# Where the attention weights are divided by their sums: before the product with v, or after it

## The chip, the core and the metric

The kernel runs on one core of a Trainium2 chip. The metric is device time in microseconds from start to end of one execution, the median of several runs. TensorE is called PE in the rows, its weight loads PEld, VectorE DVE, ScalarE ACT, GpSimd POOL, SyncE SP.

## What is computed

Three layers run one after the other over 2304 tokens (4 batches of 576). The change lies in the first of them, attention that keeps the 32 largest scores of each row:

```python
scores = scale * np.matmul(q, k.transpose(0, 1, 3, 2))       # (4, 8, 576, 576), head size 64
kth = np.partition(scores, -32, axis=-1)[..., -32:-31]
scores = np.where(scores >= kth, scores, -1000000000.0)
scores = scores - np.max(scores, axis=-1, keepdims=True)
attn = np.exp(scores)
attn = attn / (np.sum(attn, axis=-1, keepdims=True) + 1e-09)
out = np.matmul(attn, v)
x = out.transpose(0, 2, 1, 3).reshape(2304, 512)
```

The second layer is a gated one (512 to 1536 to 512, its two input matrices multiplied as a sigmoid gate and a value), the third sends each token to two of eight experts (512 to 1024 to 512) and adds their weighted results.

## The kernel before

**Order of the work.** A planner (`Plan`, L48) is handed every operation with an engine, a duration, a priority, what it depends on and which buffers it takes and returns. It plays the operations through, engine by engine, and calls the function that issues an operation at the moment at which its turn has come by these durations. So each engine's queue is in the order that the planner found, fixed when the kernel is built; on the chip each engine works its queue off in order and waits where an input or a buffer is not there yet. The number of buffers of each kind is in `CAPS` (L173): four tiles of weights (`e`), three PSUM banks `tp`, two buffers `pt` for turned weights, and so on.

**Units.** Attention is cut into units. For the first 512 queries of a batch a unit is 128 queries of two heads: two tiles of 128 x 576 scores (64 units). The last 64 queries of a batch make units of one tile, whose lower half is one head and upper half the other (16 units). There are 80 units and 144 tiles.

**The steps of a unit** (`attention`, L319), each with its engine:

- PE multiplies q and k in two fp16 halves into PSUM (L345, L348), ACT copies the scores to SBUF (`sS`, L353).
- DVE finds the 24 largest of each row (L362 to L371), POOL works out a bias (L387), ACT takes a sign (L396), POOL removes the largest (L401, L402), DVE finds the 32nd (L409), POOL notes it (L411). ACT takes the exponential of all scores (`e`, L379).
- DVE puts what is below the 32nd to zero and sums the rest of each row in the same instruction (L425, the mask); the sum lands in column 34 of `u.m`.
- POOL adds 1e-9 to the sums (L429), DVE takes the reciprocal of the two columns (L431), POOL multiplies each tile of 128 x 576 weights with it (L434).
- PE turns each tile in 128-column blocks: four blocks into one `tp` bank (L452) and the last 64 columns of both tiles into another (L471). ACT copies them to SBUF (L459, L473).
- PE multiplies v with the turned weights (L483): the result stands as 64 head columns x 128 queries for two heads, the heads in the partitions 0 to 63 and 64 to 127. ACT makes the high fp16 half of x from it (L489), DVE the low one (L492).

**Around it.** Before and beside the early units the weights of the second layer are split into fp16 halves (`weight_piece`, L279 to L290, on ACT, DVE and POOL). When all units of a chunk of 256 or 128 tokens are done, the second layer runs for it (`moe1`: L519 to L558 on PE, L526 and L533 on ACT, L529 on DVE, L536 on POOL), so that its matmuls lie between those of later units. The third layer follows when all tokens are routed (L790, L816 on PE).

Of the kernel before, what the change touches and what calls it, by code (L numbers as in the profile page):

```python
# [11 lines left out]
FT = mybir.dt.float32  # L12
# [4 lines left out]
AF = mybir.ActivationFunctionType  # L17
OP = mybir.AluOpType
# [10 lines left out]
SQ, SX, SG, SV, SO, SX2, S1, S2 = 2.0 ** 6, 2.0 ** 6, 2.0 ** 4, 2.0 ** 5, 2.0 ** 6, 2.0 ** 7, 2.0 ** 6, 2.0 ** 6  # L29
# [18 lines left out]
class Plan:  # L48
# [10 lines left out]
    def op(self, eng, dur, prio, fn, deps=(), alloc=(), use=(), lat=None, chain="", dma=False):  # L59
        o = Unit()  # L60
        o.eng, o.dur, o.prio, o.fn, o.lat = eng, dur, prio, fn, LAT[eng] if lat is None else lat
        o.alloc, o.use, o.next, o.same = list(alloc), list(alloc) + list(use), [], []
        o.n, o.id, o.dma = 0, len(self.ops), dma
        deps = list(deps)
        for t in {h.tag for h in o.alloc}:
            deps.append(self.last.get((eng, chain, t)))
            self.last[eng, chain, t] = o
        for d in deps:
            if d is not None:
                (d.same if d.eng == eng and not d.dma else d.next).append(o)  # L70
                o.n += 1
        for h in o.use:
            h.left += 1
        self.ops.append(o)
        return o
# [51 lines left out]
def attention_moe_kernel(ctx: ExitStack, tc: tile.TileContext, qT, kT, v, w_gate, w_val, w_out,  # L127
# [3 lines left out]
    V, A, P, G = nc.vector, nc.scalar, nc.tensor, nc.gpsimd  # L131
# [6 lines left out]
    ident = const.tile([128, 128], FT, name="ident")  # L138
# [26 lines left out]
    for b in range(B):  # L165
        G.iota(tok[:, 4 * b:4 * b + 4], pattern=[[128, 4]], base=b * S, channel_multiplier=1,
               allow_small_or_imprecise_dtypes=True)
        d = slice(64 * (b % 2), 64 * (b % 2) + 64)
# [2 lines left out]
    nst = const.tile([128, N // 128, E], FT, name="nst")  # L171

    CAPS = dict(st=3, w=0, tb=4, khl=5, v=5, sS=6, sg=2, m=5, y=4, e=4, pt=2, xch=2, xrem=1, th=2, g=10, x2=2,  # L173
                ps=1, tp=3, mm=3)

    def layers(fast):
        outer = ExitStack()
# [7 lines left out]
        small = p1.enter_context(tc.tile_pool(name="small", bufs=2))  # L185
        psum = p1.enter_context(tc.tile_pool(name="psum", bufs=1, space=PSUM))
        p1.enter_context(tc.manual_schedule())
        plan = Plan(CAPS)
        op = plan.op

        def tile_of(tag, shape, dt, name=None):
            pool = psum if tag in ("ps", "tp", "mm") else stage if tag == "st" else work
            return pool.tile(shape, dt, name=name or tag, bufs=CAPS[tag])
# [125 lines left out]
        def attention(u, kqr, prio):  # L319
            R = range(u.nt)  # L320
            n = 128 if u.nt == 2 else 64
            ch = u.ch
            T = [Unit() for _ in R]
# [11 lines left out]
            for t in R:  # L335
# [18 lines left out]
                a = op("PE", 0.5 if u.nt == 2 else 0.5, prio, qk, kqr.done, alloc=[hp_], use=[kqr.h])  # L354
# [27 lines left out]
            if fast:  # L382
# [8 lines left out]
                for t in R:  # L391
# [11 lines left out]
                    a = op("ACT", 0.78, prio, sg, [c2], alloc=[hg], use=[T[t].hs])  # L403
# [20 lines left out]
            def mask(t):  # L424
                return lambda: V.scalar_tensor_tensor(T[t].e, T[t].s, T[t].m[:, 31:32], T[t].e, op0=OP.is_ge, op1=OP.mult,  # L425
                                                      accum_out=T[t].m[:, 34:35])
            mk = [op("DVE", 0.75, prio, mask(t), [r4, exs[t]], use=[T[t].hs, T[t].he]) for t in R]

            iv = op("POOL", 0.12, prio - 1, lambda: G.tensor_scalar(u.m[:, :, 35], u.m[:, :, 34], 1e-9, 1.0, op0=OP.add, op1=OP.mult),  # L429
                    mk)  # L430
            iv = op("DVE", 0.08, prio - 1, lambda: V.reciprocal(u.m[:, :, 33], u.m[:, :, 35]), [iv])  # L431

            def norm(t):
                return lambda: G.tensor_scalar(T[t].e, T[t].e, u.m[:, t, 33:34], 1.0, op0=OP.mult, op1=OP.mult)  # L434
            nm = [op("POOL", 0.74, prio, norm(t), [iv], use=[T[t].he, u.hm]) for t in R]


            if u.coff == 0 and u.hp == 0:
                def opened():
                    ch.x = [work.tile([128, 4, 128 if ch.rem else 256], FH, name=f"{tag}{c}", bufs=CAPS[tag])[:, :, :ch.n]  # L440
                            for c in range(2)]
                tag = "xrem" if ch.rem else "xch"
                ch.h = plan.tile(tag)
                ch.open = op("SP", 0.0, prio, opened, alloc=[ch.h], lat=0.0)
            hpt = plan.tile("pt")
            evs = []

            def tr(t):
                def f():
                    T[t].pp = tile_of("tp", [128, 4, 128], FT)  # L450
                    for kb in range(4):
                        P.transpose(T[t].pp[:, kb, :], T[t].e[:, kb * 128:(kb + 1) * 128], ident)  # L452
                return f

            def ev(t):
                def f():
                    if t == 0:
                        u.pt = work.tile([128, NK, u.nt, 128], FT, name="pt", bufs=CAPS["pt"])
                    A.activation(u.pt[:, 0:4, t, :], T[t].pp, AF.Copy)  # L459
                return f  # L460
            for t in R:
                ht = plan.tile("tp")
                a = op("PE", 0.44, prio, tr(t), [nm[t], ch.open], alloc=[ht], use=[T[t].he])
                evs.append(op("ACT", 0.5, prio, ev(t), [a] + evs[-1:], alloc=[hpt] if t == 0 else [],
                              use=[ht] + ([hpt] if t else [])))
            h5 = plan.tile("tp")

            def tr5():
                u.p5 = tile_of("tp", [128, u.nt, 128], FT)
                for t in R:  # L470
                    P.transpose(u.p5[:64, t, :], T[t].e[:, 512:576], ident)  # L471
            a = op("PE", 0.11 * u.nt, prio, tr5, nm + [ch.open], alloc=[h5], use=[T[t].he for t in R])
            evs.append(op("ACT", 0.17 + 0.06 * u.nt, prio, lambda: A.activation(u.pt[:64, 4], u.p5[:64], AF.Copy),  # L473
                          [a, evs[0]], use=[h5, hpt]))
            hav = plan.tile("tp")

            def av():
                u.po = tile_of("tp", [128, n], FT)
                for kb in range(NK):
# [5 lines left out]
            a = op("PE", 1.31 if u.nt == 2 else 0.78, prio, av, evs + [VB[u.b, kb][2] for kb in range(NK)],  # L485
                   alloc=[hav], use=[hpt] + [VB[u.b, kb][0] for kb in range(NK)])

            def xh():
                A.activation(ch.x[0][:, u.hp, u.coff:u.coff + n], u.po, AF.Copy, scale=SX)  # L489

            def xl():
                V.scalar_tensor_tensor(ch.x[1][:, u.hp, u.coff:u.coff + n], u.po, SX,  # L492
                                       ch.x[0][:, u.hp, u.coff:u.coff + n], op0=OP.mult, op1=OP.subtract)
            d = op("ACT", 0.16, prio - 1, xh, [a], use=[hav, ch.h])
            e = op("DVE", 0.22, prio - 1, xl, [d], use=[hav, ch.h])
            ch.ready.append(e)


# [376 lines left out]
        for b in range(B):  # L875
# [3 lines left out]
            for qt in range(5) if b < B - 1 else (4, 0, 1, 2, 3):  # L879
                if qt < 4:  # L880
                    small_ch = b == 0 and qt < 2 or b == B - 1 and qt >= 2
                    if qt in (0, 2) or small_ch:
                        ch = Unit()
# [4 lines left out]
                else:  # L888
                    ch, coff = rem, 64 * (b % 2)
                    rem.rows.append((b * S + 512, 64 * (b % 2), 64 * (b % 2) + 64, 0))  # L890
                for hp in range(4):
                    u = Unit()
# [53 lines left out]
        for i, u in enumerate(units):  # L946
            if (u.b, u.hp) not in KQ:
                KQ[u.b, u.hp] = kq_ops(u.b, u.hp, 10 * i - 70, False)
            if (u.b, 0) not in VB:
                for kb in range(NK):  # L950
                    v_ops(u.b, kb, 10 * i - 20)
            attention(u, KQ[u.b, u.hp], 10 * i)
            if (u.b, u.q0, u.hp) == (1, 128, 0):
                init_out(10 * i)
            if u.ends:
                moe1(u.ch, 10 * i + PM)
                if len(routers) == ends - 2:
                    raise_counts(0, 512)
                    early = list(entered)
# [80 lines left out]
```

## Time and profile before

| | before |
|---|---|
| median of 3 runs | 1378.65 us (1378.0 to 1380.0) |
| profiled execution | 1375.23 us |
| its span | 1373.5 us |
| PE busy | 1206.5 us (88%) |
| DVE busy | 906.1 us (66%) |
| ACT busy | 798.7 us (58%) |
| POOL busy | 802.6 us (58%) |

The profile is one execution on the chip; the span runs from its first to its last instruction. Busy time is summed over the span, which holds stages of different kinds, so the shares above are averages. A group of instructions is given with its count, its busy time and the mean duration of one; a wait is put down to the instruction that released it.

### The profile page before, as it was taken

The page shows a single profiled execution, that of the slowest core. Times are in us where ns is not written, and L with a number is a line of the kernel's source. Part 1 is how long each engine was busy: PE and PEld are TensorE (multiplying, and loading weights), DVE is VectorE, ACT ScalarE, POOL GpSimd, SP SyncE. Part 2 cuts the span into 40 slices and gives each one's busy share as a digit, 9 for nine tenths or more (in the row PEclk, how much of TensorE's full clock was granted, in tenths as well). Part 3 has the DMA queues.
Part 4 walks back from the last instruction along what each step waited for, and adds up shares of the span by engine and source line. Part 5 has one row for each costly group of instructions (what it writes and reads, how often), then busy time and mean ns, then how long its engine had stood idle before and what let it go on. Part 6 is the DMA issues. An engine that isn't in the chain of part 4 may idle for free. (4 is left out here: it accounts for less than half of the span.)

```text
span 1373.5 us, 29672 instructions
## 1 busy us (share of the span) xinstructions
PE 1206.5 (88%) x10749; PEld 889.1 (65%) x10750; DVE 906.1 (66%) x3656; ACT 798.7 (58%) x1722; POOL 802.6 (58%) x1049
## 2 busy tenths in 40 slices
PE   2346578689999999999999999999999999999997
PEld 1235356466786777786867777776776666766674
DVE  5999988988989788879887884464233424334221
ACT  5767767667876767767777765563233524334221
POOL 3899998888788787768686763332221221312221
PEclk9658699799999999999999999999999999999999
DMA  8443333343003400004100013265234545343321
GB/s 190 126 125 115 102 110 87 79 120 139 16 2 94 131 2 17 9 19 125 52 2 17 10 32 104 64 192 119 46 81 125 140 82 161 82 127 93 50 47 21
DMA packets 63374, 111.79 MB, mean 81 GB/s; under 512 B 14449, under 2 KB 23793, under 8 KB 63218
## 3 DMA queue, kind: packets, MB, share of 16 engines
q1 hardware_dynamic: 53106, 89.84, 21.8%
q0 software_dynamic: 10112, 19.97, 8.0%
q8 instruction: 86, 1.41, 0.5%
q14 instruction: 70, 0.57, 0.1%
HBM read 79.58 MB, written 20.63 MB: 73 GB/s over the span
## 5 line engine op out<-in xcount | busy, mean ns | idle before, releaser
L519 PEld LDWEIGHTS <-w 128*128 128x128 f16 x3456 | 275.1, 100 | 48.9 <-issue 20.8
L519 PE MATMUL mm<-xch,w 128*128 128x256 f16 (+1 forms) x2880 | 283.4, 255 | 16.0 <-ACT th L526 7.2
L402 POOL TENSOR_TENSOR y<-sS,sg 128x576 f32<-128x576 f32 x144 | 191.2, 1328 | 9.1
L790 PE MATMUL mm<-xch,w 128*128 128x256 f16 (+1 forms) x2016 | 193.1, 256 | 0.0
L790 PEld LDWEIGHTS <-w 128*128 128x128 f16 x2016 | 170.7, 98 | 24.0
L798 DVE SCALAR_TENSOR_TENSOR g<-mm,g 128x256 f16<-128x256 f32 (+1 forms) x192 | 72.4, 379 | 160.7 <-ACT g L795 160.1
L362 DVE MAX8 cand<-sS 128x8 f32<-128x72 f32 x1152 | 166.7, 217 | 14.5 <-ACT sS L353 14.2
L558 PE MATMUL mm<-w,g 128*128 128x512 f16 x648 | 156.1, 384 | 8.0 <-POOL g L536 4.9
L761 POOL DMA_INDIRECT v<-xd,ids x40 | 42.1, 1052 | 206.9 <-DVE ws L751 185.1
L816 PEld LDWEIGHTS <-g 128*128 128x128 f16 x960 | 93.3, 98 | 98.9 <-issue 0.3
L345 PE MATMUL ps<-khl,qs 128*128 128x288 f16 x512 | 94.2, 312 | 66.1 <-ACT sS L353 41.4
L425 DVE SCALAR_TENSOR_TENSOR e<-sS,m,e 128x576 f32<-128x576 f32 x144 | 145.7, 1033 | 4.0 <-ACT e L379 3.5
L795 ACT ACTIVATE g<-mm 128x256 f16<-128x256 f32 (+1 forms) x192 | 66.4, 347 | 136.5 <-PE mm L790 130.7
L828 POOL DMA_INDIRECT out<-e,ids x40 | 63.6, 1591 | 124.4 <-ACT e L825 84.8
L536 POOL TENSOR_TENSOR g<-th,g 128x128 f16<-128x128 f32 (+1 forms) x144 | 95.8, 669 | 67.2 <-ACT g L533 66.1
L396 ACT ACTIVATE sg<-sS,m 128x576 bf16<-128x576 f32 x144 | 110.6, 769 | 38.4 <-POOL m L387 32.1
L434 POOL TENSOR_SCALAR e<-e,m 128x576 f32<-128x576 f32 x144 | 118.8, 833 | 10.4 <-DVE m L431 5.7
L452 PE MATMUL tp<-ident,e 128*128 128x128 f32 x576 | 95.4, 300 | 30.9 <-POOL e L434 29.5
L483 PE MATMUL tp<-pt,v 128*64 128x128 f32 (+3 forms) x1600 | 116.2, 281 | 5.5 <-ACT pt L459 3.6
L409 DVE MAX8 m<-y 128x8 f32<-128x584 f32 x144 | 105.5, 757 | 19.1 <-POOL y L402 18.8
L816 PE MATMUL tp<-w,g 128*128 128x512 f16 x504 | 115.1, 380 | 0.0
L483 PEld LDWEIGHTS tp<-pt,v 128*64 128x64 f32 (+1 forms) x1600 | 84.2, 141 | 40.7 <-issue 18.6
(159 smaller groups left out, 2114.4 us busy)
## 6 DMA issues: line engine op xcount, KB each, us to landing
st<-w SPq DMA_DIRECT2D x64, 512.0 KB, 4.7
khl<-st SPq DMA_DIRECT2D x48, 144.0 KB, 2.4
st<-w_gate SPq DMA_DIRECT2D x12, 512.0 KB, 3.9
st<-w_val SPq DMA_DIRECT2D x12, 512.0 KB, 4.3
st<-w_out SPq DMA_DIRECT2D x12, 512.0 KB, 3.5
st<-k_t SPq DMA_DIRECT2D x20, 288.0 KB, 3.7
st<-q_t SPq DMA_DIRECT2D x20, 288.0 KB, 3.3
xd<-x SPq DMA_DIRECT2D x18, 256.0 KB, 2.1
```

Source lines behind the costliest of these rows:

```text
L362: V.max(T[t].cand[:, 8 * c:8 * c + 8], T[t].s[:, 72 * c:72 * c + 72])
L396: A.activation(T[t].sg, T[t].s, AF.Sign, scale=-CUT[0], bias=T[t].m[:, 33:34], accum_out=T[t].m[:, 34:35])
L402: G.tensor_tensor(T[t].y[:, :S], T[t].s, T[t].sg, op=OP.mult)
L409: V.max(T[t].m[:, 24:32], T[t].y)
L425: return lambda: V.scalar_tensor_tensor(T[t].e, T[t].s, T[t].m[:, 31:32], T[t].e, op0=OP.is_ge, op1=OP.mult, accum_out=T[t].m[:, 34:35])
L434: return lambda: G.tensor_scalar(T[t].e, T[t].e, u.m[:, t, 33:34], 1.0, op0=OP.mult, op1=OP.mult)
L483: P.matmul(u.po[64 * s:64 * s + 64, :], VB[u.b, kb][1][:k, (2 * u.hp + s) * D:(2 * u.hp + s + 1) * D], rhs, start=kb == 0, stop=kb == NK - 1)
L519: P.matmul(r.ps[:, a, :], wt.t[:, a, c, kb, fo:fo + 128], ch.x[x][:, kb, :], start=i == 0, stop=i == 11)
L536: G.tensor_tensor(r.g[:, 1], r.th, r.g[:, 0], op=OP.subtract)
L558: P.matmul(r.ps, g[:, c, 128 * t:128 * t + 128], WO[f // 4].t[:, d, f % 4, :], start=f == 0 and i == 0, stop=f == 11 and i == 2)
L790: P.matmul(r.ps, W[kb].w[c][:, 0, f * 128:f * 128 + 128], q.x[x][:, kb, :], start=i == 0, stop=i == 11)
L816: P.matmul(r.ps, gs[f].g[:, c, 128 * t:128 * t + 128], W[4 + f // 2].w[d][:, f % 2, :], start=f == 0 and i == 0, stop=f == 7 and i == 2)
```

## The change

The weights stay undivided. POOL no longer multiplies the tiles, and the small sum and reciprocal go. Instead POOL writes, in one instruction per unit, a 128 x 128 tile `px` in which each row's sum plus 1e-9 is repeated (64 columns for each of two tiles, or 128 columns for one). PE turns `px` with the transposes of the last columns, into a third part of their bank. The turned tile holds, for head columns x queries, the sum of each query's row. DVE takes its reciprocal out of PSUM (128 x 128; for a unit of one tile two instructions of 64 partitions x 64 columns), and after the product with v multiplies the result with it and with the scale, into `px` in SBUF. ACT makes the high half of x from that, and the low half is now a subtraction on POOL. `px` has three buffers. Everything else is as it was.

```diff
-            iv = op("POOL", 0.12, prio - 1, lambda: G.tensor_scalar(u.m[:, :, 35], u.m[:, :, 34], 1e-9, 1.0, op0=OP.add, op1=OP.mult),
-                    mk)
-            iv = op("DVE", 0.08, prio - 1, lambda: V.reciprocal(u.m[:, :, 33], u.m[:, :, 35]), [iv])
-
-            def norm(t):
-                return lambda: G.tensor_scalar(T[t].e, T[t].e, u.m[:, t, 33:34], 1.0, op0=OP.mult, op1=OP.mult)
-            nm = [op("POOL", 0.74, prio, norm(t), [iv], use=[T[t].he, u.hm]) for t in R]
...
+            def sums():
+                u.px = small.tile([128, 128], FT, name="px", bufs=CAPS["px"])
+                G.tensor_scalar(u.px.rearrange("p (t c) -> p t c", t=u.nt), u.m[:, :, 34:35].to_broadcast([128, u.nt, 128 // u.nt]),
+                                1e-9, 1.0, op0=OP.add, op1=OP.mult)
+            hpx = plan.tile("px")
+            iv = op("POOL", 0.3, prio + 1, sums, mk + [ch.open], alloc=[hpx], use=[u.hm])
...
-                a = op("PE", 0.44, prio, tr(t), [nm[t], ch.open], alloc=[ht], use=[T[t].he])
+                a = op("PE", 0.44, prio, tr(t), [mk[t], ch.open], alloc=[ht], use=[T[t].he])
...
             def tr5():
-                u.p5 = tile_of("tp", [128, u.nt, 128], FT)
+                u.p5 = tile_of("tp", [128, 3, 128], FT)
+                P.transpose(u.p5[:, 2], u.px, ident)
                 for t in R:
                     P.transpose(u.p5[:64, t, :], T[t].e[:, 512:576], ident)
-            a = op("PE", 0.11 * u.nt, prio, tr5, nm + [ch.open], alloc=[h5], use=[T[t].he for t in R])
-            evs.append(op("ACT", 0.17 + 0.06 * u.nt, prio, lambda: A.activation(u.pt[:64, 4], u.p5[:64], AF.Copy),
+            a = op("PE", 0.11 * u.nt + 0.11, prio, tr5, mk + [iv, ch.open], alloc=[h5], use=[T[t].he for t in R] + [hpx])
+
+            evs.append(op("ACT", 0.17 + 0.06 * u.nt, prio, lambda: A.activation(u.pt[:64, 4], u.p5[:64, :u.nt], AF.Copy),
                           [a, evs[0]], use=[h5, hpt]))
+
+            def inv():
+                if u.nt == 2:
+                    V.reciprocal(u.px, u.p5[:, 2])
+                else:
+                    for s in range(2):
+                        d = slice(64 * s, 64 * s + 64)
+                        V.reciprocal(u.px[d, :64], u.p5[d, 2, d])
+            iv = op("DVE", 0.25 if u.nt == 2 else 0.34, prio, inv, [a], use=[h5, hpx])
...
+            def times():
+                u.px = u.px[:, :n]
+                V.scalar_tensor_tensor(u.px, u.po, SX, u.px, op0=OP.mult, op1=OP.mult)
+
             def xh():
-                A.activation(ch.x[0][:, u.hp, u.coff:u.coff + n], u.po, AF.Copy, scale=SX)
+                A.activation(ch.x[0][:, u.hp, u.coff:u.coff + n], u.px, AF.Copy)
 
             def xl():
-                V.scalar_tensor_tensor(ch.x[1][:, u.hp, u.coff:u.coff + n], u.po, SX,
-                                       ch.x[0][:, u.hp, u.coff:u.coff + n], op0=OP.mult, op1=OP.subtract)
-            d = op("ACT", 0.16, prio - 1, xh, [a], use=[hav, ch.h])
-            e = op("DVE", 0.22, prio - 1, xl, [d], use=[hav, ch.h])
+                G.tensor_tensor(ch.x[1][:, u.hp, u.coff:u.coff + n], u.px, ch.x[0][:, u.hp, u.coff:u.coff + n], op=OP.subtract)
+            a = op("DVE", 0.22, prio - 1, times, [a, iv], use=[hav, hpx])
+            d = op("ACT", 0.16, prio - 1, xh, [a], use=[hpx, ch.h])
+            e = op("POOL", 0.36, prio - 1, xl, [d], use=[hpx, ch.h])
```

## Rows read from the trace of the kernel before

**Rows 1.** Busy time by stage: us from:to, length, engines' busy us (instructions), clock, DMA.
```profile
core 0: us, PE busy (x) PEld busy (x) DVE busy (x) ACT busy (x) POOL busy (x), PEclk, DMA share, GB/s
34.00:100.00 66.00, 28.29 (x159) 18.18 (x158) 64.31 (x212) 45.67 (x87) 58.60 (x60) 0.56 0.40 120
...
200.00:300.00 100.00, 75.06 (x708) 55.98 (x709) 87.88 (x379) 70.31 (x155) 88.96 (x118) 0.86 0.30 81
...
34.00:300.00 266.00, 167.73 (x1500) 122.84 (x1499) 242.37 (x857) 188.65 (x400) 245.04 (x280) 0.77 0.35 104
300.00:872.00 572.00, 555.04 (x5385) 427.81 (x5384) 466.22 (x2325) 408.02 (x930) 423.54 (x634) 1.00 0.16 50
```

**Rows 2.** Waits from 34 to 300 us: waiter, releaser: us, times, longest.
```profile
PE tp L452 <- POOL e L434: 25.6, 15, 4.2
...
DVE m L431 <- POOL m L429: 3.8, 5, 1.1
```

**Rows 3.** Waits from 300 to 872 us, of PE and of DVE.
```profile
PE tp L452 <- POOL e L434: 3.8, 5, 1.4
...
PE tp L471 <- DVE xch L492: 0.4, 2, 0.2
...
DVE th L529 <- ACT th L526: 26.2, 26, 4.8
DVE m L409 <- POOL y L402: 14.3, 19, 1.2
DVE m L431 <- POOL m L429: 14.0, 17, 2.2
```

**Rows 4.** Groups by line, the reciprocal: count | busy us, mean ns | idle before.
```profile
L431 DVE RECIPROCAL m<-m 128x2 f32<-128x2 f32 x64 | 10.2, 159 | 16.2 <-POOL m L429 15.8
...
L431 DVE RECIPROCAL m<-m 128x1 f32<-128x1 f32 x16 | 2.4, 151 | 2.1 <-POOL m L429 2.0
```

**Rows 5.** Groups by line, the mask and GpSimd's work.
```profile
L425 DVE SCALAR_TENSOR_TENSOR e<-sS,m,e 128x576 f32<-128x576 f32 x144 | 145.7, 1033 | 4.0 <-ACT e L379 3.5
L434 POOL TENSOR_SCALAR e<-e,m 128x576 f32<-128x576 f32 x144 | 118.8, 833 | 10.4 <-DVE m L431 5.7 <-DVE m L368 3.7
...
L536 POOL TENSOR_TENSOR g<-th,g 128x128 f16<-128x128 f32 x72 | 41.1, 579 | 36.3 <-ACT g L533 35.7
...
L429 POOL TENSOR_SCALAR m<-m 128x2 f32<-128x2 f32 x64 | 15.4, 241 | 10.2 <-DVE e L425 5.1
...
L429 POOL TENSOR_SCALAR m<-m 128x1 f32<-128x1 f32 x16 | 3.4, 214 | 2.8 <-DVE e L425 1.6
```

**Rows 6.** Timeline of PE near 507 us (start, us), and L471's durations, min/median/max.
```profile
506.51 1.04 PE L452 MATMUL tp<-ident,e 128*128 128x128 f32 x8
507.38 0.38 PE L471 MATMUL tp<-ident,e 128*64 128x128 f32 x2
...
L471 PE MATMUL tp<-ident,e x144: 271/273/422, 33.3 to 867.3; 128*64 128x128 f32 x144
```

**Rows 7.** Groups by line, the halves of x and of the gated product.
```profile
L533 ACT ACTIVATE g<-th 128x128 f16<-128x128 f32 x72 | 21.1, 305 | 4.7 <-DVE th L529 4.2
...
L492 DVE SCALAR_TENSOR_TENSOR xch<-tp,xch 128x128 f16<-128x128 f32 x64 | 17.8, 279 | 13.9 <-ACT xch L489 13.9
L489 ACT ACTIVATE xch<-tp 128x128 f16<-128x128 f32 x64 | 17.0, 266 | 12.5 <-PE tp L483 12.5
```

**Rows 8.** Groups by line, the router's reciprocal and a subtraction of one and two columns.
```profile
L642 DVE RECIPROCAL wk<-dd 128x2 f32<-128x2 f32 x6 | 1.0, 168 | 0.2
L642 DVE RECIPROCAL wk<-dd 128x1 f32<-128x1 f32 x6 | 1.0, 164 | 0.2
...
L626 DVE TENSOR_TENSOR dd<-m 128x2 f32<-128x2 f32 x6 | 0.9, 154 | 0.0
L626 DVE TENSOR_TENSOR dd<-m 128x1 f32<-128x1 f32 x6 | 0.9, 151 | 0.0
```

**Rows 9.** The mask's durations in ns, min/median/max.
```profile
L425 DVE SCALAR_TENSOR_TENSOR e<-sS,m,e x144: 791/814/2926, 27.4 to 851.8; 128x576 f32<-128x576 f32 x144
```

**Rows 10.** Busy time of L434 alone, both stages (34 to 300, 300 to 872) together.
```profile
sum 838.00, POOL 117.31; mean POOL 58.66
```

More of the change, by code (lines that the diff above doesn't have):

```diff
@@ L173, in attention_moe_kernel @@
     CAPS = dict(st=3, w=0, tb=4, khl=5, v=5, sS=6, sg=2, m=5, y=4, e=4, pt=2, xch=2, xrem=1, th=2, g=10, x2=2,
-                ps=1, tp=3, mm=3)
+                ps=1, tp=3, mm=3, px=3)
     def layers(fast):
```

## The prediction

> **What bounds the kernel now.** I read the busy time by stage first. It has three stages [rows 1]: from 34 to 300 us attention runs beside the conversion of the second layer's weights, from 300 to 872 us attention runs beside that layer's matmuls, and after 872 us come the third layer's experts, which the change doesn't touch. In the first stage VectorE is busy 242.4 of 266 us (91.1%) and GpSimd 245.0 (92.1%), while TensorE has work for 167.7 only: two engines share the bound, and VectorE reached 64.3 of 66 us (97.4%) in the first part. In the second stage TensorE is busy 555.0 of 572 us (97.0%), VectorE 466.2 (81.5%), GpSimd 423.5 (74%): TensorE is the bound, and the others have room. The chain of waits in the page says almost nothing here, so I went to the waits by engine: in the first stage TensorE stands 25.6 us, in 15 waits, for the normalized weights of GpSimd (L434), and VectorE's longest group of waits is 3.8 us [rows 2]; in the second stage L434 costs TensorE 3.8 us [rows 3]. So the removed step is a real wait early and almost none late.
>
> **The change part by part.** There are 80 units (a pair of heads for 128 queries, or for the last 64): 64 of two tiles and 16 of one, 144 tiles in all; the counts of the reciprocal put 1 unit before 34 us, 20 in the first stage and 59 in the second (64 and 16 instances in all [rows 4]).
>
> *GpSimd.* Out go one normalization of each tile (144 x 0.833 us) and the sum with 1e-9 (64 x 0.241 and 16 x 0.214) [rows 5]: 119.9 + 18.9 = 139 us. In come the widened sums, one 128x128 instruction per unit. Between a tensor_scalar of 2 columns (0.241) and of 576 columns (0.833) its price by width is about 0.37; and the low part of x moves here from VectorE: its nearest row is the 128x128 subtraction L536, 0.579 us [rows 5] (the 64-column one of the 16 one-tile units I take at 0.45). That is 64 x 0.95 + 16 x 0.82 = 74 us. GpSimd is relieved of 65 us in all, and of about 1 us per two-tile unit, so some 18 us in the first stage.
>
> *TensorE.* One more transpose per unit. Eight transposes in a row take 1.04 us and two take 0.38 with a single one at 0.273 [rows 6], so each that follows another costs 0.11 us: 59 x 0.11 = 6.5 us in the stage that TensorE bounds, with nothing to hide it. The 21 early ones fall into idle time.
>
> *ScalarE.* The high part of x is read from SBUF and not from PSUM: 0.305 (L533) against 0.266 us (L489) [rows 7]. 64 x 0.04 = 2.5 us on an engine busy 408 of 572 us [rows 1]: nothing. If it were not covered it would be those 2.5 us.
>
> *VectorE.* The product with the reciprocals takes the place of the old low part; both are scalar_tensor_tensor over 128x128 from PSUM, 0.279 us [rows 7], so that is even. The reciprocal is the disputed term: it was 128x2 and becomes 128x128 (for one-tile units two of 64x64). No row has a wide reciprocal. From below its price is a one-pass instruction of that shape, 0.279 us. From above it is the reciprocal's own slope: 128x1 takes 0.151 and 128x2 0.159 [rows 4], 8 ns a column, which makes 0.159 + 126 x 0.008 = 1.17 us; the other reciprocal, L642, has 164 and 168 ns [rows 8], 4 ns a column, 0.67 us. Less than nothing is excluded, since the instruction replaced costs 0.159 and is narrower. A subtraction beside it, L626, grows by 3 ns from one column to two [rows 8], so a slope from so few columns is weak. I take 1.17 us, from the row that is the same operation with the most instances, 64 and 16. The two half-width ones then cost 2 x (0.151 + 63 x 0.008) = 1.31. Net per unit: 1.17 - 0.16 = 1.01, or 1.31 - 0.15 = 1.16 us; 64 x 1.01 + 16 x 1.16 = 83 us more on VectorE, 21 in the first stage and 61 in the second. By the lower price it is 64 x 0.12 + 16 x 0.27 = 12 us.
>
> The Trainium skill, VectorE: DVE Perf Modes, section "Walkthrough: the 8-slice pipeline in each mode", says that the reciprocal is an iterative divide with a repeat count of 8, at a clock of 0.96 GHz; an estimate from that page is 128 x 8 / 0.96 GHz = 1.07 us of work for the wide one, and the sum by it stays within some 10 us of VectorE time of the one taken here. The slope of L431 (8 ns a column) agrees with that rule, that of L642 (4 ns) only halfway, and a wide reciprocal near the 0.279 us of the one-pass row would refute it.
>
> A relief stands against this. The mask L425 has a median of 814 ns and a mean of 1033, with a maximum of 2926 [rows 5, 9]: it is drawn out where it meets GpSimd's work, 144 x 0.219 = 31.5 us in all. The normalization is 117.3 of GpSimd's 668.6 busy us of both stages [rows 1, 10], 18%, so about 6 us may go, 3 in each stage; between 0 and 10.
>
> *New waits.* The fifth transpose now waits for the widened sums on GpSimd, where it waited for two normalizations; they come no later than those. The bank that it fills is held until VectorE has done the reciprocal, and not only until ScalarE has copied it. There are three such banks; behind a late one stand TensorE's next transposes, the product with v and the scores of the next unit, and the whole loop waits for those. Today's nearest row is TensorE's wait for VectorE's L492, which frees a bank of the same kind: 0.4 us in two waits in the second stage [rows 3]. From below I take nothing, from above 0.2 us a unit, 12 us in the second stage, since VectorE gets fuller; I take half, 6 us. The end of a chunk is one hop longer (VectorE, ScalarE, GpSimd in place of ScalarE, VectorE), some 0.6 us, covered by the other matmuls except after the last chunk.
>
> **The sum.** First stage: VectorE has 242.4 + 21 - 3 = 260 us of work. At its best share (97.4%) that takes 267 us, +1; at today's (91.1%) 286, +20. GpSimd's relief speaks for the first, that VectorE meets more waits on its own queue for the second; I take +10. Second stage: +6.5 for the transposes, -2 for half of the 3.8 us of waits on L434 (the other half passes to the mask), +6 for banks: +10.5, with ends of +2.7 and +16. VectorE then has 466 + 61 - 3 = 524 of some 582 us, 90%. Third stage: nothing. Together +20.5, ends +4 and +36. The profiled execution took 1375.23 us (span 1373.5), so 1396 for it; it lies 3.4 us below the median 1378.65, from which the same sum gives 1399. I say 1398.
>
> **The rivals.**
> *A cheap reciprocal: faster.* If the wide reciprocal goes through in about one pass (0.28 us), VectorE gains only 3 us in the first stage, which the relief pays back. Then TensorE's 25.6 us of waits on L434 go and what is late next is VectorE: at 97.4% its 242 us fill 249, so at most -17 us; I take -8. The second stage has +6.5 - 3.8 = +2.7. The sum is -5, from -14 to +3: 1364 to 1382, likeliest 1373. It decides at the reciprocal's price: with VectorE midway between its two shares (94.3%) the first stage has 250.8 - 239.4 = 11.4 us of room, less 2.7 for the second stage, over 20 units 0.43 us, so below a reciprocal of about 0.6 us the kernel is faster. For it speak the weak slope and the L642 pair; against it the L431 pair.
> *The dear reciprocal is swallowed.* VectorE waits 26.2 + 14.3 + 14.0 us in its longest groups of the second stage [rows 3]; later arrivals shorten those waits. With +1 in the first stage and +2.7 in the second, about 1382 (1379 to 1385). For it: room of 18% late; against it: there is none early.
> *VectorE paces both stages.* Its work of 708.6 + 83 - 6 = 786 us, at the share that it keeps where three engines are nearly full (87.9 of 100 us between 200 and 300 [rows 1]), takes 894 instead of 838 us: +56. The planner orders the queues with 0.25 us for the wide reciprocal, so ready TensorE work would stand behind late units. I price it at 1414 to 1435. Against it: much of TensorE's work in the second stage is the second layer's for chunks whose attention is long done.
>
> **How the numbers follow.** Forecast (1384 to 1414): 0.50. Cheap reciprocal: 0.25. Swallowed: 0.12. VectorE paces all: 0.13. What a measurement of this kernel can tell from no change is about 0.2%, 2.8 us. Faster: most of the cheap case, 0.19. Same: the rest of it and half of the swallowed case, 0.12. Slower: 0.69. The range leaves out about the lower 0.10 of the cheap case and 0.08 of the last: 1370 to 1424.
>
> **What would show it.** Right: the group of the wide reciprocal has a mean near 1.1 us, VectorE's busy time rises by 70 to 85 us and GpSimd's falls by about 65; TensorE's transposes take no wait on GpSimd any more but wait on the mask; the second layer ends 15 to 25 us later, and the time after it stays at 500 us. Wrong: a mean of 0.3 us for the reciprocal, or TensorE's share of the second stage above 97% at a first stage that is shorter than 266 us.

## The result, and the profile after

The changed kernel takes 1396.6 us (median, 1392.0 to 1400.6), the kernel before 1379.3 (1378.0 to 1381.3) in runs beside it: a ratio of 1.0123, with a 95% interval of 1.0088 to 1.0157. It is slower, by 12 to 22 us. The forecast was 1398. The sum was right; of its three stages one had the wrong sign and one was half of what it is, and the experiments below show which terms. Ratios and intervals here and below leave out two executions far from all others, one of 2493 us of the last experiment and one of 4212 us of the kernel before.

The groups of the new and the touched instructions (columns as in [rows 4]), in the changed kernel. L479 and L483 are the reciprocals, L440 the widened sums, L469 their turn, L474 ScalarE's copy of the turned last columns (out of the same bank as the turned sums), L506 the low half of x, L451 the transposes of the weights:

```profile
L425 DVE SCALAR_TENSOR_TENSOR e<-sS,m,e 128x576 f32<-128x576 f32 x144 | 139.8, 991 | 3.3 <-ACT e L379 2.2
L451 PE MATMUL tp<-ident,e 128*128 128x128 f32 x576 | 92.1, 295 | 62.2 <-DVE e L425 54.2 <-POOL good L411 5.8 <-DVE m L368 1.5
...
L479 DVE RECIPROCAL px<-tp 128x128 f32<-128x128 f32 x64 | 60.8, 950 | 23.6 <-PE tp L471 11.3 <-ACT pt L474 7.8 <-ACT dd L675 3.9
...
L506 POOL TENSOR_TENSOR xch<-px,xch 128x128 f16<-128x128 f32 x64 | 35.7, 558 | 15.7 <-ACT xch L503 15.1
L440 POOL TENSOR_SCALAR px<-m 128x128 f32<-128x128 f32 x80 | 27.1, 339 | 34.7 <-DVE e L425 21.1 <-DVE m L368 7.4 <-ACT xch L503 0.8
L469 PE MATMUL tp<-ident,px 128*128 128x128 f32 x80 | 24.9, 311 | 23.1 <-POOL px L440 19.3 <-DVE ohsum L662 1.1 <-DVE px L500 0.9
L474 ACT ACTIVATE pt<-tp 64x256 f32<-64x256 f32 x64 | 23.8, 372 | 19.4 <-DVE px L479 12.2 <-PE tp L471 6.1 <-DVE dd L655 0.9
...
L503 ACT ACTIVATE xch<-px 128x128 f16<-128x128 f32 x64 | 19.4, 303 | 11.3 <-DVE px L500 10.2 <-POOL g L550 1.0
...
L483 DVE RECIPROCAL px<-tp 64x64 f32<-64x64 f32 x32 | 17.7, 552 | 1.4 <-ACT pt L474 1.1
```

The wide reciprocal takes 0.950 us, against 0.159 for the narrow one [rows 4]; before it VectorE stands idle for 23.6 us in sum, because its queue is in a fixed order: 11.3 us until the transposes are done, 7.8 until ScalarE has copied the last columns (L474). The wait goes the other way too: L474 stands 12.2 us for the wide reciprocal. In the plan the two are free of each other, but they read the same bank, and in this trace none of the 96 reciprocals runs at the same time as such a copy. In the kernel before this copy never waits for VectorE. The transposes of the weights wait 54.2 us for the mask, where they waited for the normalization [rows 2].

For the stages I cut both traces at the same piece of work and not at the same time: the first 25 units are done when the product with v has run 500 matmuls (20 per unit), and the third layer begins with its first matmul. Counts of the product's matmuls, first the kernel before, then the changed one (us from:to, PE and PEld busy and instructions), and after each the third layer's first and last matmul of its first expert:

```profile
0.00:350.00 350.00, 42.07 (x500) 30.26 (x500) 0.82 0.40 117
L790 PE MATMUL mm<-xch,khl x288: 218/272/273, 911.0 to 966.6; 128*128 128x256 f16 x96, 128*128 128x128 f16 x48
```
```profile
0.00:343.00 343.00, 42.47 (x500) 31.23 (x500) 0.84 0.41 119
L804 PE MATMUL mm<-xch,khl x288: 219/272/273, 926.4 to 980.6; 128*128 128x256 f16 x96, 128*128 128x128 f16 x48
```

The first 25 units are done 7 us earlier, the third layer begins 15.4 us later: the part between grew by 22 us, from 561 to 583. (Cut after 20 units, near the end of the forecast's first stage, the gain is 3 us, 299.4 to 296.2, and the rest grows by 19.) Its busy times (columns as in [rows 1]), before and after:

```profile
350.00:911.00 561.00, 541.52 (x5366) 418.86 (x5366) 444.39 (x2162) 393.15 (x900) 399.83 (x596) 1.00 0.17 48
```
```profile
343.00:926.00 583.00, 555.55 (x5432) 429.08 (x5431) 486.42 (x2208) 401.46 (x909) 357.26 (x562) 0.99 0.16 46
```

TensorE is busy 14 us longer there, with 66 more instructions, and idle 27.5 in place of 19.5 us; VectorE's work rose from 444 to 486 us and is still only 83% of the part. The third layer takes 469 us in this trace and 463 in the trace of before. All traces of the experiments but one (466) have 467 to 470, among them those of kernels that are faster than the one before, so I don't count those 6 us as the change's; the profiled execution of before was a short one.

### The profile page after: what moved, and what is told of

It reads as the page before. It is cut to its first block, busy times and chain, and to the rows that moved or that the text cites. A ratio compares the mean times of both kernels' runs of the same rounds, so it can differ in the third digit from the quotient of the medians.

```text
span 1395.8 us, 29894 instructions
## 1 busy us (share of the span) xinstructions
PE 1225.0 (88%) x10829; PEld 904.0 (65%) x10830; DVE 951.2 (68%) x3672; ACT 802.6 (58%) x1722; POOL 734.4 (53%) x985
## 5 line engine op out<-in xcount | busy, mean ns | idle before, releaser
L451 PE MATMUL tp<-ident,e 128*128 128x128 f32 x576 | 92.1, 295 | 62.2 <-DVE e L425 54.2
L425 DVE SCALAR_TENSOR_TENSOR e<-sS,m,e 128x576 f32<-128x576 f32 x144 | 139.8, 991 | 3.3 <-ACT e L379 2.2
L550 POOL TENSOR_TENSOR g<-th,g 128x128 f16<-128x128 f32 (+1 forms) x144 | 92.7, 648 | 73.9 <-ACT g L547 67.5
L451 PEld LDWEIGHTS tp<-ident,e 128*128 128x128 f32 x576 | 69.5, 151 | 79.3 <-DVE e L425 38.4
```

## The experiments

All ratios are against the kernel before, run beside; 0.1% is 1.4 us. Kernels that alter the result are named so in their expectations. Lines of code left out are marked `...`. With every edit the planner plays its operations through anew, so the order of the queues changes too; only the run with the planner's durations changes the order and nothing else. What was left in question was the price of each part: V (the reciprocal's time on VectorE), T (the transpose's on TensorE), Q (the planner's wrong duration), B and T-wait (the bank held, the waits for the widened sums).

**The reciprocal taken before the sums are widened.**

```diff
+            rc = op("DVE", 0.08, prio - 1, lambda: V.reciprocal(u.m[:, :, 35], u.m[:, :, 34]), mk, use=[u.hm])
...
-                    V.reciprocal(u.px, u.p5[:, 2])
+                    V.tensor_copy(u.px, u.p5[:, 2])
...
```

> The reciprocal is taken of the two sums per row, before they are widened (128x2 on VectorE, as in the kernel before), and the turned tile is only copied out of PSUM, a one-pass instruction of some 0.28 us instead of the reciprocal's 0.95. The addition of 1e-9 is left out. Everything else, the extra transpose too, is as in the changed kernel (1396.6 us, against 1379.3 before). Theory V, VectorE's time for the wide reciprocal makes the kernel slower: 80 units get about 0.5 us of VectorE back, 40 us in all, and the time falls to 1375 to 1386 us. Theory T, the extra transpose on TensorE makes it slower (TensorE's busy time before the third layer rose by 13.5 us and its idle time by 1.5): 1390 to 1397 us.

1383.1 us, ratio 1.0009 (0.9987 to 1.0032): as V had it. The same chain with a copy in place of the reciprocal is level with the kernel before; the reciprocal's width is worth 1.14% here, some 16 us. The copy takes 0.285 us, and VectorE stands ahead of it as long as it did, 14.7 us for ScalarE's copy out of the same bank (L475) and 8.2 for the transposes:

```profile
L480 DVE COPY px<-tp 128x128 f32<-128x128 f32 x64 | 18.2, 285 | 28.9 <-ACT pt L475 14.7 <-PE tp L472 8.2 <-issue 3.6
```

So these waits of VectorE don't cost much by themselves; with 0.67 us more work behind each the kernel is 16 us slower.

**No turn.**

```diff
-                P.transpose(u.p5[:, 2], u.px, ident)
...
-                    V.reciprocal(u.px, u.p5[:, 2])
+                    V.reciprocal(u.px, u.px)
...
```

> The extra transpose is left out and the wide reciprocal is taken in place of the unturned tile in SBUF, so that each result is divided by the sum of another query; the fifth transpose waits no more for the widened sums. VectorE's work is as in the changed kernel. Theory V: 1391 to 1398 us. Theory T: 80 transposes of 0.11 to 0.17 us and the 19 us in which TensorE waits for the widened sums go, some of that again lost to the next wait: 1378 to 1387 us.

1376.0 us, ratio 0.9948 (0.9928 to 0.9968): better than T's range, and V missed it. With the full reciprocal on VectorE, but no turn, the kernel is faster than before. So neither term alone explains the loss. (The reciprocal also reads SBUF here, and no longer holds the bank.)

**No division.**

```diff
-            iv = op("POOL", 0.3, prio + 1, sums, mk + [ch.open], alloc=[hpx], use=[u.hm])
...
-                P.transpose(u.p5[:, 2], u.px, ident)
...
-            iv = op("DVE", 0.25 if u.nt == 2 else 0.34, prio, inv, [a], use=[h5, hpx])
...
-                V.scalar_tensor_tensor(u.px, u.po, SX, u.px, op0=OP.mult, op1=OP.mult)
+                V.tensor_scalar(u.px, u.po, SX / 32.0, None, op0=OP.mult)
...
```

> No sums, no extra transpose, no reciprocal: the product with v is multiplied with a constant on VectorE (0.28 us), and the two halves of x are made as in the changed kernel. The division is left out. It measures what taking the normalization off GpSimd is worth by itself. If the relief is real in the first stage (the units of the changed kernel were some 7 us early by 340 us): 1365 to 1374 us. If it is worth nothing: 1376 to 1381 us.

1369.6 us, ratio 0.9907 (0.9879 to 0.9934): the relief is real, 0.93% or 13 us; that is what the change gains where the division costs nothing. It comes early, as the count of the product's matmuls shows: 25 units are done after 332 us, in place of 350. Some of TensorE's other work is put off by that (46 instructions fewer from 34 us to there), and the part behind it is 8 us longer.

```profile
0.00:332.20 332.20, 45.86 (x500) 33.02 (x500) 0.84 0.43 123
```

**The planner told the true durations.**

```diff
-            iv = op("DVE", 0.25 if u.nt == 2 else 0.34, prio, inv, [a], use=[h5, hpx])
+            iv = op("DVE", 0.95 if u.nt == 2 else 1.1, prio, inv, [a], use=[h5, hpx])
```

> The changed kernel, with the planner told 0.95 us for the wide reciprocal and 1.1 us for the two narrow ones, in place of 0.25 and 0.34; the work is the same, only the order of the queues differs. Theory Q, the queues are out of order because the planner thinks VectorE freer than it is: 1382 to 1391 us. Theories V and T: 1393 to 1400 us.

1397.0 us, ratio 1.0101 (1.0073 to 1.0129): Q falls. The loss doesn't come from the planner's wrong duration for the reciprocal, and another order of all queues left the time as it was.

**The kernel before, with one more transpose and nothing else.**

```diff
-                u.p5 = tile_of("tp", [128, u.nt, 128], FT)
+                u.p5 = tile_of("tp", [128, 3, 128], FT)
+                P.transpose(u.p5[:, 2], ident, ident)
...
```

> The kernel before, with one more transpose per unit (of the constant identity, into the third part of the bank of the last columns) and nothing else: 80 transposes that wait for nothing new. Theory T-time, the extra transpose costs by TensorE's own time: 0.11 to 0.17 us each, 59 of them in the stage that TensorE bounds, so 6 to 13 us above the kernel before (1380.9): 1387 to 1394. Theory T-wait, it costs by what it waits for (the widened sums) and by its bank, which VectorE frees late: 1379 to 1385.

1391.8 us, ratio 1.0066 (1.0047 to 1.0086): T-time. 80 transposes that wait for nothing cost 9 us, 0.11 us each if all of them are counted and 0.15 if only the 59 of the second stage are.

**The bank emptied by ScalarE, the reciprocal in SBUF.**

```diff
+            a = op("ACT", 0.27 if u.nt == 2 else 0.4, prio, out5, [a], use=[h5, hpx])
...
-            iv = op("DVE", 0.25 if u.nt == 2 else 0.34, prio, inv, [a], use=[h5, hpx])
+            iv = op("DVE", 0.25 if u.nt == 2 else 0.17, prio, inv, [a], use=[hpx])
```

> The changed kernel, but ScalarE copies the turned tile out of PSUM (some 0.27 us more per unit on ScalarE) and the wide reciprocal is then taken in SBUF, in place; VectorE's work is the same, the bank is freed without it. Theory B, the wide reciprocal holds the bank and that makes transpose and reciprocal dearer together (27 us) than apart (13.5 and 6.4): 1385 to 1391 us. If the bank doesn't matter: 1394 to 1401 us.

1399.2 us, ratio 1.0133 (1.0110 to 1.0156): B's range is missed: that VectorE holds the bank does not by itself make the changed kernel slow. What the bank costs isn't measured alone, since the edit also puts ScalarE's copy as one more hop between turn and reciprocal, and the one-tile units' two reciprocals become one of 128x64 (0.540 us in place of two of 0.552).

**The turn moved to the product.**

```diff
-                P.transpose(u.p5[:, 2], u.px, ident)
...
+                z = tile_of("tp", [128, 2, 128], FT)
+                u.po, u.pz = z[:, 0, :n], z[:, 1]
+                P.transpose(u.pz, u.px, ident)
...
```

> The changed kernel, but the widened sums are turned just before the product with v and into the product's bank, in place of before the last columns: TensorE waits no more for the sums ahead of its fifth transposes, and their bank is freed by ScalarE alone. Number of transposes, reciprocal and product as in the changed kernel. Theories T-wait and B: 1379 to 1388 us. Theory T-time: 1392 to 1398 us.

1397.4 us, ratio 1.0120 (1.0095 to 1.0146): outside the range of T-wait and B. TensorE's waits for the widened sums (8.5 us in the second part of the changed kernel) are gone from its longest groups, and it waits for the mask in their place. But the edit brings in a wait of its own. Of the 27.2 us that VectorE stands ahead of the reciprocal 26.1 are for the product with v (L497), which writes the same bank: no unit's reciprocal starts between the end of its turn and the end of its product. One wait is gone and another is in the chain, so this run doesn't tell what the wait for the sums cost. First TensorE's wait for the mask between 340 and 927 us (columns as in [rows 2]), then the reciprocal's group:

```profile
PE tp L451 <- DVE e L425: 6.0, 9, 1.5
...
L485 DVE RECIPROCAL px<-tp 128x128 f32<-128x128 f32 x64 | 60.9, 951 | 27.2 <-PE tp L497 26.1 <-POOL y L402 0.9
```

**Late turn, narrow reciprocal, the copy on ScalarE.** A candidate for a better kernel: VectorE's work as before, GpSimd relieved.

```diff
-                    V.reciprocal(u.px, u.p5[:, 2])
+                    A.activation(u.px, u.pz, AF.Copy)
...
```

> As the late turn, but the reciprocal is taken of the two sums before they are widened, and ScalarE copies the turned tile out of PSUM: VectorE's work is that of the kernel before, GpSimd is relieved, TensorE has 80 more transposes. The addition of 1e-9 is left out. Without division the kernel took 1369.6 us; with 59 transposes of 0.11 to 0.17 us in TensorE's stage 6.5 to 10 us more by T-time: 1376 to 1380 us; with nothing by T-wait: 1369 to 1373 us.

1384.0 us, ratio 1.0013 (1.0000 to 1.0026): a miss by 4 us, no better than the narrow reciprocal with its copy on VectorE. What the relief gives, the turn, the widened sums and the copy take back.

**The kernel before, with a wide reciprocal that nobody waits for.**

```diff
+                    V.reciprocal(px, onef)
...
+            op("DVE", 0.25 if u.nt == 2 else 0.34, prio, inv, [a], alloc=[hpx])
```

> The kernel before, with one wide reciprocal per unit more on VectorE (of a constant, into a tile that nobody reads, queued behind the fifth transpose as in the changed kernel) and nothing else. Theory L, the reciprocal costs by its time on VectorE, whoever waits for it: some 76 us more of VectorE work, 19 of it in the first stage where VectorE is busy 91%: 1387 to 1396 us. Theory D, it costs because the product and a bank wait for it: 1379 to 1384 us.

1402.2 us, ratio 1.0158 (1.0137 to 1.0179): beyond L's range, and D falls. VectorE's time alone costs 22 us in the kernel before. The first part is no longer for it: 25 units are done after 349.6 us, as before, though VectorE is busy 297 of 316 us there; but TensorE has done 31 instructions fewer by then (1887 against 1918), which come later. The loss shows in the part that TensorE bounds, 18 us of it in this trace. This kernel's busy times in both parts (columns as in [rows 1]), and the kernel before in the first:

```profile
34.00:350.00 316.00, 212.69 (x1887) 158.34 (x1886) 297.42 (x1091) 222.92 (x474) 282.96 (x337) 0.79 0.35 109
350.00:929.00 579.00, 550.59 (x5395) 424.09 (x5394) 492.11 (x2236) 395.12 (x902) 400.68 (x598) 0.99 0.16 46
```
```profile
34.00:350.00 316.00, 216.18 (x1918) 159.13 (x1917) 284.40 (x1069) 224.79 (x477) 286.45 (x339) 0.81 0.35 109
```

In the second part VectorE is 85% busy. TensorE's idle time has gone from 19.5 to 28.4 us, with no new wait in the program, and its busy time by 9 us, with 29 instructions more. The new idle time is mainly the second layer's matmuls standing for ScalarE (L539, `th`) and the transposes standing for the normalization. Waits in the second part (columns as in [rows 2]), before and in this kernel:

```profile
PE mm L519 <- ACT th L526: 3.0, 4, 1.3
PE tp L452 <- POOL e L434: 2.4, 4, 0.9
```
```profile
PE mm L532 <- ACT th L539: 7.8, 6, 2.3
PE tp L454 <- POOL e L436: 6.7, 8, 2.6
```

**Both additions to the kernel before, nobody waiting.** The two edits above together.

> The kernel before with both additions, the transpose of a constant and the reciprocal of a constant, and nobody waiting for either. Theory L: the price of both together exceeds the sum of the two alone, as it did in the changed kernel (27 us against 13.5 and 6.4): 1400 to 1412 us. Theory D: the transpose's 10 us alone, 1389 to 1394 us.

1399.2 us, ratio 1.0131 (1.0110 to 1.0152): just below L's range, far above D's. Beside the reciprocal the transpose, worth 9 us alone, costs nothing that can be measured. In these kernels, each with its own order of the queues, the two prices don't add.

**The row turned by DMA.**

```diff
+                    nc.sync.dma_start(rd[u.i + t:u.i + t + 1, :].rearrange("o p -> p o"), u.m[:, t, 35:36])
...
+                    nc.sync.dma_start(u.px[64 * s:64 * s + 64, :n], src.to_broadcast([64, n]))
...
```

> A version without the extra transpose: the reciprocal of the two sums per row is taken before anything is widened (128x2 on VectorE), written to DRAM as a row by a DMA of SyncE and read back over 64 partitions by another, in place of the widened sums and their turn; VectorE then multiplies the product with it, and the halves of x are made as in the changed kernel. The addition of 1e-9 is left out. If the two transfers are there before VectorE comes to the product, the time is that of the kernel without division (1369.6 us) and little more: 1369 to 1376 us. If they come late, or hold up the loads of q and k behind them in SyncE's queue: 1383 to 1400 us.

1567.2 us, ratio 1.1351 (1.1328 to 1.1375): far worse than its worse case. SyncE's queue stands ahead of a unit's read until its write has landed, 79 times and 5.0 us a time, and VectorE stands for the read (waits as in [rows 2]):

```profile
DVE px L500 <- DMA px<-rd: 185.2, 44, 10.8
...
SPq L450 <- DMA rd<-m: 394.3, 79, 9.4
```

**Both loads as in the changed kernel, without the chain between them.** The kernel without the turn, plus a transpose of the identity.

```diff
+                P.transpose(u.p5[:, 2], ident, ident)
...
```

> The version without the turn (1376.0 us: wide reciprocal in SBUF of the unturned tile, each result divided by the sum of another query), with a transpose of the constant identity added at the place of the turn, which waits for nothing. VectorE's and TensorE's work are those of the changed kernel (1396.6), only the dependences widened sums to transpose and transpose to reciprocal are missing. If the two loads by themselves make the changed kernel slow: 1393 to 1399 us. If 10 us are the transpose's time, as in the kernel before with only the transpose, and the rest the waits of the chain: 1384 to 1389 us.

1384.3 us, ratio 1.0021 (1.0004 to 1.0037): the second answer. TensorE and VectorE have the changed kernel's instructions, and 1.0% or 14 us of its loss are missing. What is missing are the dependences sums to turn to reciprocal, and with them the shared bank: the reciprocal reads SBUF, and ScalarE's copy L474 waits no more for VectorE. VectorE's wait ahead of the reciprocal falls from 23.6 to 5.1 us. The second row counts the product's matmuls: with both loads but without the chain 25 units are done after 332 us, as without any division, and with the chain after 343. So in these traces 11 us of the chain's price arise there.

```profile
L479 DVE RECIPROCAL px<-px 128x128 f32<-128x128 f32 x64 | 60.2, 941 | 5.1 <-POOL px L440 5.0
```
```profile
0.00:331.70 331.70, 43.53 (x500) 31.19 (x500) 0.80 0.42 123
```

**Put together.** One path of edits leads from the kernel before to the changed one, each step a difference of two ratios:

| step | from, to | price |
|---|---|---|
| no normalization, low half on GpSimd | 1.0000, 0.9907 | -13 us |
| widened sums and wide reciprocal, free of the turn | 0.9907, 0.9948 | +6 us |
| a transpose that waits for nothing | 0.9948, 1.0021 | +10 us |
| the chain: sums, turn, reciprocal out of the shared bank, product | 1.0021, 1.0123 | +14 us |

The steps add up because they are differences along one path; the prices depend on the path, and with both intervals taken together each of the last three is uncertain by some 4 to 5 us. The reciprocal costs 22 us on top of the kernel before, 6 (with the widened sums) on top of the one without division, and 16 as the last link of the chain (1.0009 to 1.0123).

The wide reciprocal behind the turn is slow in all four kernels that have it, each with another order of the queues: 1396.6 to 1399.2 us (changed, true durations, bank emptied by ScalarE, late turn). With a narrow reciprocal and a turn at either place it is 1383.1 and 1384.0, with the wide one free of the turn 1376.0 and 1384.3. So the loss is the wide reciprocal in the chain, and not the luck of one order; the single prices may hold some of the order's.

## Why the prediction was right, and where only its sum was

**The price of the reciprocal: right in kind.** It was put at 1.17 us from L431's slope, with 0.67 by L642's; it is 0.950, and the pair of 64 columns 1.10 in place of 1.31. From 64 to 128 columns it grows by 398 ns, 6.2 a column: the two slopes of 8 and 4 ns stood on either side. The repeat count of 8 in the Trainium skill (VectorE: DVE Perf Modes, "Walkthrough: the 8-slice pipeline in each mode"), taken as 8 cycles a column at that page's 0.96 GHz, makes an estimate of 8.3 ns; the trace has a quarter less, and the trace decides. VectorE's busy time rose by 45 us in all (906.1 to 951.2) and not by 70 to 85: 78.5 of reciprocals less 12.6 of the old one are 66, and many other groups took a little less, the mask 5.9. The forecast had 6 for the mask, but that agreement is luck: in the run with the true durations, which has the same instructions, the mask takes 151.0 us, more than before (145.7), and VectorE is busy 964.6. A relief of the mask isn't shown.

**GpSimd: right.** 0.339 us for the widened sums (0.37 forecast), 0.558 for the low half (0.579), and 68 us of relief (65).

**The first stage: wrong in sign.** The step that failed reads "VectorE has 242.4 + 21 - 3 = 260 us of work. At its best share (97.4%) that takes 267 us ...; at today's (91.1%) 286": it took a share of 91% for a bound. The kernel with an idle reciprocal shows that it is none for the units: 13 us more of VectorE's work fit into the same 316 us, at the price of 3.5 us of TensorE's work put off. The other engine at 92%, GpSimd, was on the path, through the waits of L452 that I had read [rows 2] and then left out of this stage's sum: without division the same 25 units take 18 us less. With both loads but without the chain they still do; with the chain 7 are left.

**The second stage: right in sign, half the size.** +10.5 was forecast, +22 measured (+19 from the end of the 20th unit). Three terms:
- The transposes, 6.5 us, measured as 9 and 10 us where they wait for nothing, and as nothing beside the idle reciprocal.
- The banks, 6 us: that step failed. In the changed kernel TensorE's waits for a bank that VectorE frees come to 2.7 us in this part, and emptying the bank by ScalarE didn't make the kernel faster. What the shared bank does was not in the forecast: ScalarE's copy and the reciprocal wait for each other (12.2 and 7.8 us).
- "VectorE then has ... 90%" was taken as room. VectorE's work costs time in this stage at a share of 85%. With the reciprocal alone TensorE's idle time went from 19.5 to 28.4 us, ahead of matmuls and transposes that depend on other engines. That these come late because VectorE does, whatever its mean share is, is argued from the fixed order of the queues. This term was missing.

**"They come no later than those"** on the widened sums: wrong in part. TensorE waits 19.3 us for L440 in the changed kernel. What that costs isn't shown by itself: where the turn comes late, TensorE stands for the mask in its place, but the reciprocal then waits for the product.

**The third stage: nothing**, as forecast.

**The rivals.** A cheap reciprocal was to make the kernel faster, 1373 us, and to decide at 0.6 us. With a copy of 0.285 us in its place the kernel is level with the one before. So that rival had the right cause for the loss and the wrong sign: its first stage was near (25 units are done after 339.8 us, 10 early, 8 forecast), but the second is 12 us longer and not 2.7. The dear reciprocal swallowed (1379 to 1385) is out for the changed kernel, but nearly holds without the chain (6 us). VectorE pacing both stages (1414 to 1435) is out by the time, and the planner's wrong duration as its reason by the run with the true ones. That the forecast hit 1398 is luck: two errors met, -7 in place of +10 early, +22 in place of +10.5 late.

**Open.** Why the prices don't add is not settled. The chain's 14 us are shown as a difference of two kernels with the same instructions on TensorE and VectorE, but in another order. Which link makes them is open: the wait of the turn for the sums, the reciprocal's waits (17 to 27 us in the four forms with the wide one behind the turn, 5 in the one without), or ScalarE's copy waiting for the reciprocal in the shared bank. The narrow form has the same waits of VectorE at a ratio of 1.0009; its ScalarE copy waits 6.0 us for VectorE, in place of 13.9 (both shapes). No run lifts that wait alone. TensorE's busy time also differs between traces by more than the few instructions that moved seem to account for: 541.5 us for 5366 instructions and 550.6 for 5395 in the second part of the kernel before without and with an idle reciprocal, with granted clocks of 1.00 and 0.99. How much of that is the clock and how much the modelled ends was not told apart.

## What to carry to other kernels

A division that moves from the operand to a smaller result isn't cheaper if the divisor must first be brought into the result's layout: count what widens, turns and inverts it, and invert before widening, where 2 columns do in place of 128. A high share of busy time is not a bound and a lower one is not room: an engine at 90% took 13 us more work and its units were done no later, and more work on the same engine at 79% made the part behind it 18 us longer. Price an extra link in such a chain by trying it, since the prices of two additions needn't add. And look for the waits that the plan doesn't name: here two engines that read one bank stood for each other.

## What the runs showed of the hardware

The reciprocal on VectorE costs 6.2 ns a column of fp32 (0.552 us for 64 x 64, 0.950 for 128 x 128), from PSUM and from SBUF alike (0.941); 64 x 64 and 128 x 64 both take 0.540 us in SBUF. 128 x 128 takes over three times a copy of the same shape (0.285 us). ScalarE's and VectorE's reads of one PSUM bank never ran at the same time in the changed kernel (96 reciprocals, 80 copies). Where rows of 128 single fp32 values went to DRAM and back in one SyncE queue, the queue stood 5.0 us on average until a unit's write had landed, and the kernel went from 1381 to 1567 us.
